# Wide attention with its score tile in 3 + 1 PSUM banks, its exponential in two instructions, and a new instruction order

## The chip, the core and the metric

One NeuronCore of a Trainium2 chip runs the whole program. The metric is the device time in microseconds (us) of one execution, as the median of several. The engines run side by side and meet only at semaphores: TensorE (PE in the profile) multiplies matrices into PSUM, ScalarE (ACT) computes exponentials and copies, VectorE (DVE) copies and does elementwise work, GpSimd (POOL) copies within SBUF and issues DMAs, SyncE (SP) issues DMAs. PSUM is eight banks, each of 512 fp32 numbers on each of 128 partitions; a matmul's result of 512 columns fills a bank.

## The reference, cut to what matters

Two attentions read the same input `x` (2048 x 576), and a gate mixes them.

```python
# A: 64 segments of 32 rows, one after the other; 8 memory rows go from one to the next
for s in range(n_seg):
    h = concatenate([mem, xs])                 # 8 + 32 rows
    q, k, v = h @ Wq, h @ Wk, h @ Wv           # 32 heads of 128
    p = softmax(where(mask, q @ k.T * scale, -1e9))
    o = (p @ v) @ Wo
    mem, out_s = o[:, :M], o[:, M:]
# B: plain attention over all 2048 rows, 32 heads of 18
b = softmax(q @ k.T * Dh ** -0.5) @ v @ wo
return g * a + (1 - g) * b                     # g = sigmoid(sum(x * gate_w))
```

A is a recurrence: segment s + 1 needs the output of segment s. B, the wide attention, has no such chain but 32 score matrices of 2048 x 2048, and so nearly all of the exponentials.

## The kernel before, in words

**Stages.** First x is transposed and B's q, k and v are projected (`xt`, `pq`, `pv`, L580 to L751) and written to DRAM. Then A's 64 segments run one after the other, and B's attention is laid between their steps. Last come B's output product and the mix (L1667, L1683).

**The wide attention.** B's heads are taken in 8 groups of 4, the queries in 4 chunks of 512, the keys in 16 blocks of 128: 32 x 16 = 512 *visits* (loops over `gq` and `kb`). A visit has three steps:

- `sb` (L906): four matmuls, one for each head, on four row tiles of PE, into one tile `sb` of 128 x 4 x 512 fp32, which is four PSUM banks;
- `ex` (L915): one exponential on ACT over all 2048 columns into the SBUF tile `etb` (two buffers);
- `ob` (L924): four matmuls on four column tiles that add the values, weighted, into `ob`, a bank which stays open for 16 visits.

There is one `sb` tile, so the scores of the next visit can't start before the exponential of this one has ended. The other three banks are a common pool, `pb`, from which everything else takes its PSUM.

**A segment of the recurrence.** `Q`, `K`, `V` (L1249) project the 40 rows in two halves each, copies bring them to SBUF (`tm`, L520 on ACT or L522 on DVE), q and k are turned by a DMA transpose (L1340) and copied (L1349). For each half follow `ph` (scores, L1364 and L1372), an exponential on ACT (L1382), `sm` (sums, L1396), a reciprocal (L1408), `bc` (spread, L1422), a product (L1433), `po` (values, L1444, two pool banks at once), copies `ot`, and `op` (output product, L1157). `fo` (L1501) forms the next segment's memory rows. The last 8 rows of each segment don't feed the recurrence and are projected ahead (`la`, L994 and L998).

**What sets the order.** No scheduler of the compiler does: the class `Plan` does, while the program is built. Each step is added with an engine (or a choice of two), a modelled duration, its dependences, a priority, and the tokens (PSUM banks, buffers) that it takes and gives back. `run` then places steps one at a time on the engine that is free first, by priorities that are weighed anew at each segment by a number from the list `TURNS`. Each engine then runs its steps in exactly that order. The steps of PE have a *mode* (row, col, tall, full: how the array is tiled). Where the plan leaves PE idle for long, it places filler matmuls (`warm`, L877, zeros added to the open `ob`). A visit may not run ahead of the recurrence by more than a share: each later `sb` also depends on a step of some segment (`seg_gate`).

Of the kernel before, what the change touches and what calls it, by code (L numbers as in the profile page):

```python
# [10 lines left out]
FP32 = mybir.dt.float32  # L11
BF16 = mybir.dt.bfloat16
ACT = mybir.ActivationFunctionType
# [41 lines left out]
]  # L55
RANK = dict(RANKS[0])
TURNS = [
    7943601, 1705423, 4803270, 706643, 9682343, 8274704, 7872199, 5071302, 3371851, 3273616, 4640218, 4495581,
    5292743, 3779423, 6345635, 4968460, 6155672, 9072000, 3125259, 7567437, 7423799, 1541135, 1346239,
    9763583, 3431211, 1894600, 9694456, 752252, 1250417, 1686256, 2185370, 1863123, 9947015, 7980497, 9379971,  # L60
    9658427, 1322130, 8351749, 3131186, 1013253, 3672070, 1863938, 4951784, 5438165, 9176668, 3266295,
    9739128, 9697170, 3740036, 3789983, 7951007, 3736728, 7365096, 2930305, 1889627, 3969272, 8605176, 949486,
    6403568, 927810, 5200634, 8113583, 1742827, 48857, 9352253,
]
FACTORS = (0.02, 0.1, 0.25, 0.4, 0.55, 0.7, 0.85, 1.0, 1.2, 1.5, 1.9, 2.4, 3.0, 4.0, 6.0, 10.0)
KNOBS = ("switch", "near", "early", "wait", "gap", "cool")
# [10 lines left out]


def kind_of(name):
    if re.match(r"(sb|ob|ex)\d+\.", name):  # L80
        return name[:2]
    if re.match(r"l[ae]\d", name):
        return name[:2] + ("v" if name.split(".")[1] == "2" else "q")
    m = re.match(r"([a-zA-Z]+\d?)\.\d+(?:\.\d+)?$", name) or re.match(r"([a-zA-Z]{2})\d+$", name)
    return m.group(1) if m else "x"
# [20 lines left out]
class Plan:  # L106
# [57 lines left out]
    def add(  # L164
        self, name, engs, dur, fn, deps=(), prio=5.0, mode=None, take=(), give=(), tail=0.0, dmas=0, kb=0.0,
        use=None, pairs=4,
    ):
        op = Op(name, engs, dur, fn, deps, prio, mode, take, give, tail)
        op.dmas, op.kb = dmas, kb
        op.pairs = pairs  # L170
        op.kind = self.kinds.setdefault(kind_of(name), len(self.kinds))
        op.use = self.ARRAY.get(mode) if use is None else use
        op.seq = len(self.ops)
        op.slots = {}
        self.ops.append(op)
        return op
# [179 lines left out]
def act_time(n):  # L356
    return (n + 205) / 1200.0
# [3 lines left out]
def kernel(  # L361
# [15 lines left out]
    nc = tc.nc  # L377
    P = nc.NUM_PARTITIONS
# [12 lines left out]
    QC = 512  # L391
# [16 lines left out]
    scale_b = float(DhB) ** -0.5  # L408
# [6 lines left out]
    plan = Plan()  # L415
    add = plan.add
# [29 lines left out]
    for jj in range(2):  # L446
        nc.vector.memset(bsel[64 * jj:64 * jj + 64, jj:jj + 1], 1.0)
    nc.gpsimd.affine_select(
        out=veil[0:64, M:L], in_=veil[0:64, M:L], pattern=[[1, seg]],
# [3 lines left out]
        out=veil[0:64, 0:M], in_=veil[0:64, 0:M], pattern=[[0, M]],  # L453
        compare_op=ALU.is_gt, fill=-30000.0, base=L, channel_multiplier=-1,
    )
    for j in range(4):
        r = slice(32 * j, 32 * j + 32)
# [41 lines left out]
    ps_s = ctx.enter_context(tc.tile_pool(name="ps_s", bufs=1, space=psum))  # L499
# [1 line left out]
    ps_a = ctx.enter_context(tc.tile_pool(name="ps_a", bufs=1, space=psum))  # L501
    plan.tokens_of("sb", 1)
    plan.tokens_of("ob", 1)
    plan.tokens_of("pb", 3)
    plan.tokens_of("etb", 2)

    def bank(shape, dt, name, k=0):
        return ps_a.tile(shape, dt, name=name, tag=f"pb{plan.slot('pb', k)}")
# [48 lines left out]
    box = {}  # L557
# [229 lines left out]
    def gate(e):  # L787
        pgs = bank([P, NT], FP32, "pgs")
        for n in range(NT):
            for c in range(NF + 1):  # L790
# [7 lines left out]
             prio=0.45, mode="full", take=("pb",), pairs=80)  # L798
# [38 lines left out]
    k_of, v_of, q_of = {}, {}, {}  # L837
# [35 lines left out]
    last_vi = last_va = None  # L873
# [16 lines left out]
    for gq in range(GB * NQC):  # L890
        RANK.update(RANKS[gq // 8])
        g, qc = divmod(gq, NQC)
        load_q(gq)
        for kb in range(NKB):
            c = 4 * g + kb // KC
            o = (kb % KC) * P
            if qc == 0 and kb % KC == 0:
                load_k(c)
                load_v(c)

            def visit(e, c=c, gq=gq, o=o, kb=kb):
                box["sb", gq, kb] = sb = ps_s.tile([P, 4, QC], FP32, name="sb")
                kc, qt_ = kring[c % NKR], qring[gq % NQR]
                for j in range(4):
                    r = slice(32 * j, 32 * j + 32)
                    nc.tensor.matmul(  # L906
                        sb[:, j, :], lhsT=kc[r, o:o + P], rhs=qt_[r, :], start=True, stop=True,
                        tile_position=(32 * j, 0),
                    )

            vi = add(f"sb{gq}.{kb}", "PE", 0.216, visit, [k_of[c], q_of[gq], last_vi], prio=-0.6 if gq < 2 else 0.0, mode="row", take=("sb",))

            def expo(e, gq=gq, kb=kb):
                box["etb", gq, kb] = etb = given(bint, "etb", [P, 4, QC], BF16)
                nc.scalar.activation(out=etb[:, :, :], in_=box["sb", gq, kb][:, :, :], func=ACT.Exp, scale=scale_b)  # L915

            ex = add(f"ex{gq}.{kb}", "ACT", act_time(2048), expo, [vi], prio=0.0, take=("etb",), give=(("sb", vi, 0),))

            def values(e, c=c, gq=gq, kb=kb, o=o):
                if kb == 0:  # L920
                    box["ob"] = ps_o.tile([P, QC], FP32, name="ob")
                ob, vc, etb = box["ob"], vring[c % NVR], box["etb", gq, kb]
                for j in range(4):
                    nc.tensor.matmul(  # L924
                        ob[32 * j:32 * j + 32, :], lhsT=vc[:, o + 32 * j:o + 32 * j + 32], rhs=etb[:, j, :],
                        start=(kb == 0), stop=(kb == NKB - 1), tile_position=(0, 32 * j), skip_group_check=True,
                    )
                if kb == NKB - 1:
                    box["ob", gq] = ob

            va = add(
                f"ob{gq}.{kb}", "PE", 0.216, values, [ex, v_of[c], last_va], prio=-0.5 if gq < 2 else RANK["ob"], mode="col",
                take=("ob",) if kb == 0 else (), give=(("etb", ex, 0),),
            )
            visits[gq, kb] = (vi, ex, va)
            last_vi, last_va = vi, va
            if kb == 0:
                plan.opens.add(va)
            if kb == NKB - 1:
                plan.closes.add(va)  # L940
            if kb == 0:
                first_va = va
            if kb == NKB - 1:
                visits["quse", gq] = vi
            if qc == NQC - 1 and kb % KC == KC - 1:
                visits["kuse", c], visits["vuse", c] = vi, va

        NBK = QC // 32

        def f_turn(e, gq=gq):  # L950
            box["tq", gq] = tq = bint.tile([P, NBK, 32], FP32, name="tq")
            nc.vector.transpose(out=tq[:, :, :].rearrange("p b e -> p (b e)"), in_=box["ob", gq][:, :])

        def f_rec(e, gq=gq):
            box["rtb", gq] = rtb = bint.tile([P, NBK, 1], FP32, name="rtb")
            nc.vector.reciprocal(out=rtb[:, :, :], in_=box["tq", gq][:, :, DhB:DhB + 1])

        def f_mul(e, gq=gq):
            box["tn", gq] = tn = bint.tile([P, NBK, 32], BF16, name="tn")
            nc.vector.tensor_tensor(  # L960
                out=tn[:, :, :], in0=box["tq", gq][:, :, :],
                in1=box["rtb", gq][:, :, :].to_broadcast([P, NBK, 32]), op=ALU.mult,
            )

        def f_back(e, gq=gq):
            box["stage", gq] = stage = bint.tile([P, QC], BF16, name="stage", bufs=2)
            nc.vector.transpose(out=stage[:, :], in_=box["tn", gq][:, :, :].rearrange("p b e -> p (b e)"))  # L967

        prev = fin_state.get("back")
        f1 = add(f"ft{gq}", "DVE", 0.7, f_turn, [va, prev], prio=0.5, give=(("ob", first_va, 0),))  # L970
        f2 = add(f"fr{gq}", "DVE", 0.26, f_rec, [f1], prio=RANK["fin"])
        f3 = add(f"fm{gq}", "DVE", 0.7, f_mul, [f2], prio=RANK["fin"])
        store2 = stages.get(gq - 2)
        f4 = add(f"fb{gq}", "DVE", 0.7, f_back, [f3, store2], prio=RANK["fin"])
        fin_state["back"] = f4
        if gq < GB * NQC - 1:
            def f_store(e, gq=gq, g=g, qc=qc):
                by_head(otd, g, slice(qc * QC, (qc + 1) * QC), box["stage", gq], True, queue(e))

            stages[gq] = add(f"fs{gq}", *carrier(4, True), f_store, [f4], prio=0.9, dmas=4, kb=90)  # L980
        else:
            stages[gq] = f4
# [196 lines left out]
    for s in range(n_seg):  # L1179
# [45 lines left out]
        def ld_v(e, s=s):  # L1225
# [8 lines left out]
            prio=0.76, dmas=2, kb=64,  # L1234
# [70 lines left out]
        for hf in range(2):  # L1305
# [3 lines left out]
            for a, ev_a in ((0, eq), (1, ek)):  # L1309
                if hf in ON_PE:  # L1310
                    def turn_pe(e, hf=hf, s=s, a=a):
# [11 lines left out]
                        take=("pb",), give=(("tm", ev_a, 0),), pairs=16,  # L1323
# [14 lines left out]
                def turn(e, hf=hf, s=s, a=a):  # L1338
# [5 lines left out]
                    give=(("tm", ev_a, 0),), dmas=1, kb=128,  # L1344
                )

                def ct(e, hf=hf, s=s, a=a):
# [8 lines left out]
                    prio=RANK["ct"], give=(("tt", t_, 0),),  # L1356
# [31 lines left out]
            def sm(e, hf=hf, s=s):  # L1388
                box["pss", s, hf] = ps = bank([P, 6], FP32, "pss")
                for k, o in enumerate(CH):  # L1390
# [4 lines left out]
                    for i in range(4) if SM_COL else ():  # L1395
# [7 lines left out]
                     mode="col" if SM_COL else "full", take=("pb",), use=0.05, pairs=12 if SM_COL else 3)  # L1403
# [33 lines left out]
            def pso(e, hf=hf, s=s):  # L1437
# [3 lines left out]
                for r in range(8):  # L1441
                    for jj in range(2):
# [8 lines left out]
                     give=(("tm", evx, 0),))  # L1451
# [292 lines left out]
```

## Time and profile before

| | |
|---|---|
| median of 3 runs | 1467.89 us (1466.71 to 1469.4) |
| the profiled execution, a fourth one | 1462.26 us |
| its span, first to last instruction | 1460.4 us |
| PE, ACT, DVE, POOL busy | 1364.7, 1055.9, 793.9, 556.3 us |
| exponential of a visit on ACT | 512 x 1877 ns |
| ACT idle just before it | 317.0 us |
| first `sb`, last `sb` start | 63.6 us, 1445.2 us |
| filler matmuls on PE | 768 in column tiles (192 fours), 2 whole |

All other numbers are of the profiled execution. A busy share counts the time in which an instruction of the engine is recorded; on PE the records overlap, since one matmul starts while the one before still drains. A group's line gives line number, engine, operation, output and input tiles, shapes and count, then busy time and mean ns of one, then how long the engine stood idle just before such an instruction and who ended that. `[0.61 <-ACT etb L915]` in a timeline means: idle for 0.61 us, until ACT's instruction of line 915 that writes `etb` was done.

### The profile page before, as it was taken

To read this page: it belongs to the slowest core of one execution; us is meant where nothing else is said; L and a number is where in the kernel's file an instruction comes from. 1 tells how busy PE (TensorE), PEld (TensorE's weight loads), DVE (VectorE), ACT (ScalarE), POOL (GpSimd) and SP (SyncE) were. 2 spreads that over 40 slices of the span, in tenths; PEclk is the share of its full clock that TensorE was granted. 3 is DMA by queue.
4 is the path that set the end of the run, shared out by engine and by line. 5 is a ranking of instruction groups with operands and counts; after the bars stand their busy time and mean duration, and the time that the engine had idled before them with its cause. 6 is when DMAs were issued, how large, how long until landed. Compare 5 with 4: busy or idle time off the path is not lost.

```text
span 1460.4 us, 79019 instructions
## 1 busy us (share of the span) xinstructions
PE 1364.7 (93%) x35726; PEld 760.8 (52%) x35735; DVE 793.9 (54%) x1862; ACT 1055.9 (72%) x773; POOL 556.3 (38%) x1194
## 2 busy tenths in 40 slices
PE   6889999999999999999999999999998999988998
PEld 4446455555555545555555455555554454544544
DVE  6434555656566555555555565555554555555554
ACT  2257677777877777777777777887777778777884
POOL 6323336333453335333454334541444342523210
PEclk9999999999999999999999999999999999999999
DMA  8986534333324233333233333333343323332261
GB/s 251 323 273 197 106 71 76 68 60 74 74 70 74 57 69 76 66 59 72 56 86 67 67 67 68 82 63 65 62 94 63 57 53 57 71 59 56 48 166 59
DMA packets 343420, 130.75 MB, mean 90 GB/s; under 512 B 296943, under 2 KB 329159, under 8 KB 343083
## 3 DMA queue, kind: packets, MB, share of 16 engines
q1 hardware_dynamic: 314771, 81.20, 27.7%
q0 software_dynamic: 27088, 43.31, 10.6%
q8 instruction: 279, 4.57, 1.4%
q10 hardware_dynamic: 1224, 1.20, 0.2%
q14 instruction: 58, 0.48, 0.1%
HBM read 52.74 MB, written 30.86 MB: 57 GB/s over the span
## 4 chain that ended last, share of the span: by engine, by line
PE 60%; DMA 6%; DVE 6%; ACT 6%; issue 4%; POOL 1%; ACTq 0%; DVEq 0%; POOLq 0%
PE pvv L1249 22%; PE acc L1157 8%; PE sb L906 8%; PE ob L924 7%; DMA tt<-tm 5%; ACT etb L915 5%; PE pv L994 3%; PE pso L1444 2%; PE ob L877 2%; PE po L1667 1%; PE prb L1422 1%; DVE tm L522 1%; DMA v_sb<-tm 1%; PE psh L1372 1%; PE pw L1501 1%
## 5 line engine op out<-in xcount | busy, mean ns | idle before, releaser
L915 ACT ACTIVATE etb<-sb 128x2048 bf16<-128x2048 f32 x512 | 961.2, 1877 | 317.0 <-PE sb L906 304.0
L522 DVE CAST tm<-pvv 128x512 bf16<-128x512 f32 x364 | 251.1, 690 | 255.2 <-PE pvv L1249 248.2
L1249 PEld LDWEIGHTS <-ht 128*32 128x32 bf16 x7680 | 202.1, 96 | 194.8 <-DVE ht L1511 19.8
L906 PE MATMUL sb<-qch,kch 32*128 32x512 bf16 x2048 | 204.0, 385 | 13.9 <-ACT etb L915 10.7
L924 PE MATMUL ob<-etb,vch 128*32 128x512 bf16 x2048 | 203.4, 388 | 1.0 <-issue 0.6
L1157 PE MATMUL acc<-wo,ot 128*32 128x144 bf16 x8192 | 165.8, 227 | 9.5 <-issue 7.8
L1157 PEld LDWEIGHTS <-ot 128*32 128x32 bf16 x8192 | 136.3, 96 | 34.6 <-issue 14.5
L1249 PE MATMUL pvv<-wk_m,ht 128*32 128x512 bf16 x2048 | 142.2, 379 | 0.3 <-DVE ht L1511 0.3
L1249 PE MATMUL pvv<-wq_m,ht 128*32 128x512 bf16 x2048 | 137.4, 380 | 3.8 <-DVE ht L1511 0.6
L1249 PE MATMUL pvv<-wv_m,ht 128*32 128x512 bf16 x2048 | 140.0, 379 | 0.4 <-DVE tm L522 0.4
L906 PEld LDWEIGHTS <-kch 32*128 32x128 bf16 x2048 | 59.7, 91 | 140.4 <-issue 114.3
L522 DVE CAST ot<-pso 128x320 bf16<-128x320 f32 x197 | 90.9, 486 | 72.4 <-PE pso L1444 70.4
L826 POOL DMA_DIRECT2D qch<-qtd x120 | 61.8, 522 | 108.2 <-PE sb L906 107.5
L1349 DVE COPY qk<-tt 128x512 bf16<-128x512 bf16 x256 | 80.7, 322 | 32.5 <-DMA tt<-tm 29.5
L924 PEld LDWEIGHTS <-vch 128*32 128x32 bf16 x2048 | 53.4, 93 | 81.2 <-issue 76.3
L1200 POOL COPY ht<-xg 128x96 bf16<-128x96 bf16 x64 | 18.0, 281 | 203.1 <-PE pvv L1249 201.9
L1288 POOL COPY v_sb<-tm 32x512 bf16<-32x512 bf16 x68 | 42.8, 629 | 126.3 <-DVE tm L522 111.6
L826 POOL DMA_DIRECT2D otd<-stage x124 | 62.9, 514 | 58.5 <-DVE stage L967 35.2
L1433 DVE TENSOR_TENSOR et<-et,prb 128x320 bf16<-128x320 bf16 x128 | 62.0, 484 | 36.4 <-PE prb L1422 34.1
L826 POOL DMA_DIRECT2D kch<-ktd x112 | 57.2, 518 | 59.0 <-PE sb L906 49.4
L522 DVE CAST vl<-pv 128x512 bf16<-128x512 f32 x86 | 58.7, 685 | 34.2 <-PE pv L994 23.4
L1382 ACT ACTIVATE et<-psh 128x320 bf16<-128x320 f32 x128 | 55.7, 435 | 13.3 <-PE psh L1372 12.2
(152 smaller groups left out, 1853.4 us busy)
## 6 DMA issues: line engine op xcount, KB each, us to landing
xl<-qkd SPq DMA_DIRECT2D x64, 128.0 KB
v_sb<-tm SPq DMA_DIRECT2D x256, 32.0 KB
qkd<-vl POOLq DMA_DIRECT2D x48, 128.0 KB, 2.3
wo<-in_A_Wo_dram POOLq DMA_DIRECT2D x4, 1152.0 KB
vgd<-vt SPq DMA_DIRECT2D x32, 128.0 KB
wv_m<-in_A_Wv_dram POOLq DMA_DIRECT2D x4, 1024.0 KB, 7.0
wq_m<-in_A_Wq_dram POOLq DMA_DIRECT2D x4, 1024.0 KB, 7.5
wk_m<-in_A_Wk_dram POOLq DMA_DIRECT2D x4, 1024.0 KB, 8.1
```

The costliest lines, as they stand in the source:

```text
L522: nc.vector.tensor_copy(out=out_of(), in_=in_of())
L826: dma(out=rows_, in_=pads) if out else dma(out=pads, in_=rows_)
L906: nc.tensor.matmul(sb[:, j, :], lhsT=kc[r, o:o + P], rhs=qt_[r, :], start=True, stop=True, tile_position=(32 * j, 0),)
L915: nc.scalar.activation(out=etb[:, :, :], in_=box["sb", gq, kb][:, :, :], func=ACT.Exp, scale=scale_b)
L924: nc.tensor.matmul(ob[32 * j:32 * j + 32, :], lhsT=vc[:, o + 32 * j:o + 32 * j + 32], rhs=etb[:, j, :], start=(kb == 0), stop=(kb == NKB - ...
L994: nc.tensor.matmul(out_, lhsT=lw, rhs=rw, start=(c == 0), stop=(c == NF))
L1157: nc.tensor.matmul(acc[32 * j:32 * j + 32, :], lhsT=o[:, slot, t0:t0 + CT], rhs=wo[:, h, RW * j:RW * j + RW], start=(first and s_ == 0), s ...
L1249: nc.tensor.matmul(pv[32 * j:32 * j + 32, :], lhsT=ht[:, cc, :], rhs=rw, start=(c == 0), stop=(c == NF), tile_position=(0, 32 * j), skip_g ...
L1288: move(out=opened["v_sb"][64 * (j // 2):64 * (j // 2) + CT, o:o + 512], in_=tm[32 * j:32 * j + CT, :],)
L1349: eng.tensor_copy(out=opened["qk"][:, hf, a, 0:16 * L].rearrange("p (j i t) -> p j i t", i=4, t=L)[:, :, :, 0:CT], in_=box["tt", s, a, hf] ...
L1382: nc.scalar.activation(out=opened["et", hf][:, :], in_=box["psh", s, hf][:, :], func=ACT.Exp, scale=scale_a)
L1433: nc.vector.tensor_tensor(out=et[:, :], in0=et[:, :], in1=box["prb", s, hf][:, :], op=ALU.mult)
```

## The change

The score tile has three banks instead of four. The fourth head's scores go to a bank `sp` of the common pool, which grows from three to four. The exponential is two instructions: three heads (1536 columns), which gives back the three banks, then one head (512), which gives back the pool's bank. The values wait for both. The list `TURNS` is another one, so the order of all steps on all engines differs. Lines after the change stand 6 lower than before from L936 on (L1249 becomes L1255), `sb` is L907, `ob` L930, the two exponentials L916 and L920.

```diff
@@ TURNS = [
-    7943601, 1705423, 4803270, 706643, 9682343, 8274704, 7872199, 5071302, 3371851, 3273616, 4640218, 4495581,
...
+    7483491, 5720459, 7783898, 6678073, 6223742, 3115698, 6578494, 0, 354389, 7990747, 1981828, 1088679,
...
-    plan.tokens_of("pb", 3)
+    plan.tokens_of("pb", 4)
...
-                box["sb", gq, kb] = sb = ps_s.tile([P, 4, QC], FP32, name="sb")
+                box["sb", gq, kb] = sb = ps_s.tile([P, 3, QC], FP32, name="sb")
+                box["sp", gq, kb] = sp = bank([P, QC], FP32, "sp")
...
                     nc.tensor.matmul(
-                        sb[:, j, :], lhsT=kc[r, o:o + P], rhs=qt_[r, :], start=True, stop=True,
+                        sb[:, j, :] if j < 3 else sp[:, :], lhsT=kc[r, o:o + P], rhs=qt_[r, :], start=True, stop=True,
                         tile_position=(32 * j, 0),
                     )
-            vi = add(f"sb{gq}.{kb}", "PE", 0.216, visit, [k_of[c], q_of[gq], last_vi], prio=-0.6 if gq < 2 else 0.0, mode="row", take=("sb",))
+            vi = add(f"sb{gq}.{kb}", "PE", 0.216, visit, [k_of[c], q_of[gq], last_vi], prio=-0.6 if gq < 2 else 0.0, mode="row", take=("sb", "pb"))
...
-                nc.scalar.activation(out=etb[:, :, :], in_=box["sb", gq, kb][:, :, :], func=ACT.Exp, scale=scale_b)
-
-            ex = add(f"ex{gq}.{kb}", "ACT", act_time(2048), expo, [vi], prio=0.0, take=("etb",), give=(("sb", vi, 0),))
+                nc.scalar.activation(out=etb[:, 0:3, :], in_=box["sb", gq, kb][:, :, :], func=ACT.Exp, scale=scale_b)
+
+            def expo4(e, gq=gq, kb=kb):
+                etb = box["etb", gq, kb]
+                nc.scalar.activation(out=etb[:, 3, :], in_=box["sp", gq, kb][:, :], func=ACT.Exp, scale=scale_b)
+
+            ex = add(f"ex{gq}.{kb}", "ACT", act_time(1536), expo, [vi], prio=0.0, take=("etb",), give=(("sb", vi, 0),))
+            ey = add(f"ey{gq}.{kb}", "ACT", act_time(512), expo4, [ex], prio=0.01, give=(("pb", vi, 0),))
...
             va = add(
-                f"ob{gq}.{kb}", "PE", 0.216, values, [ex, v_of[c], last_va], prio=-0.5 if gq < 2 else RANK["ob"], mode="col",
+                f"ob{gq}.{kb}", "PE", 0.216, values, [ex, ey, v_of[c], last_va], prio=-0.5 if gq < 2 else RANK["ob"], mode="col",
                 take=("ob",) if kb == 0 else (), give=(("etb", ex, 0),),
             )
```

The modelled durations in `add` and `act_time` steer the order only; nothing of them runs. Counted in the two programs as they are built:

| | before | after |
|---|---|---|
| matmuls on PE | 35735 | 35767 |
| fillers (fours) | 192 | 200 |
| changes of PE's mode | 1356 | 1382 |
| exponentials of the wide attention | 512 | 1024 |
| copies `tm` on DVE, on ACT | 364, 20 | 343, 41 |
| copies `vl` on DVE, on ACT | 86, 10 | 78, 18 |
| copies `v_sb` on DVE, on POOL | 188, 68 | 208, 48 |

## The prediction

> **What bounds the kernel now.** First the page: span and busy shares, then the slices.
>
> ```profile
> span 1460.4 us, 79019 instructions
> PE 1364.7 (93%) x35726; PEld 760.8 (52%) x35735; DVE 793.9 (54%) x1862; ACT 1055.9 (72%) x773; POOL 556.3 (38%) x1194
> ...
> PE   6889999999999999999999999999998999988998
> ACT  2257677777877777777777777887777778777884
> ```
>
> The tensor engine is the only one near full, from slice 4 to the end; ScalarE stands at seven tenths throughout. An engine at a constant seven tenths is either paced by another or waits in every round for the same thing, so next the groups and the waits of the wide attention.
>
> ```profile
> L915 ACT ACTIVATE etb<-sb 128x2048 bf16<-128x2048 f32 x512 | 961.2, 1877 | 317.0 <-PE sb L906 304.0
> L906 PE MATMUL sb<-qch,kch 32*128 32x512 bf16 x2048 | 204.0, 385 | 13.9 <-ACT etb L915 10.7
> L924 PE MATMUL ob<-etb,vch 128*32 128x512 bf16 x2048 | 203.4, 388 | 1.0 <-issue 0.6
> ```
>
> Each waits for the other: the exponential for the scores (304 us, on an engine with room), the scores for the exponential (10.7 us shown, on the engine without room). The timeline shows the ring, first on PE, then on ACT.
>
> ```profile
> 1140.10 0.39 PE L906 MATMUL sb<-qch,kch 32*128 32x512 bf16 x4
> 1140.43 0.40 PE L924 MATMUL ob<-etb,vch 128*32 128x512 bf16 x4
> 1140.74 1.18 PE L1157 MATMUL acc<-wo,ot 128*32 128x144 bf16 x64
> 1142.54 0.40 PE L906 MATMUL sb<-qch,kch 32*128 32x512 bf16 x4 [0.61 <-ACT etb L915]
> ```
>
> ```profile
> 1140.61 1.88 ACT L915 ACTIVATE etb<-sb 128x2048 bf16<-128x2048 f32 x1
> 1143.04 1.88 ACT L915 ACTIVATE etb<-sb 128x2048 bf16<-128x2048 f32 x1 [0.56 <-PE sb L906]
> ```
>
> The four score banks are one tile. Its ring takes 0.51 us from the scores' start to the exponential's start, 1.88 for the exponential, 0.05 back to PE: 2.43 (here 1142.54 - 1140.10 = 2.44). PE stood 0.61 us, with ready work behind the waiting matmul. The windows say where this is worst.
>
> ```profile
> 876.00:1022.00 146.00, 141.79 (x4048) 83.66 (x4047) 78.87 (x188) 113.98 (x88) 57.96 (x124) 1.00 0.34 70
> 1022.00:1168.00 146.00, 133.23 (x3804) 73.20 (x3800) 76.59 (x180) 110.65 (x81) 62.56 (x131) 1.00 0.37 69
> 1168.00:1314.00 146.00, 132.46 (x3992) 72.12 (x3988) 76.17 (x182) 114.68 (x86) 57.38 (x123) 1.00 0.34 60
> ```
>
> The first number after the length is PE's busy time: 142 of 146 us up to 1022, 133 and 132 after that.
>
> **What the Trainium skill says.** "Perfetto Trace Analysis", Identifying the Most-Contended Engine: matmul busy time is no good measure of what is left, since matmuls overlap. The trace agrees: a wait of 0.1 us hides under the end of the matmul before, so I count from start to start below. The same page, Identifying Performance Opportunities: a bubble that repeats can mean that PSUM has no room for the next tile; the 0.56 us above is such a bubble (no gap between two successive exponentials was shorter than 0.55). The same page, Optimizing Scalar/DVE Operations: where ScalarE is not full but makes others wait, instructions may be broken up, at about 51 ns of engine time each for PSUM; the trace gives 65, worked out below, and that is used. "TensorE: Matmul & The Clock Gate", Part 3: matmuls start and end strictly in order, so all that is queued behind a waiting one waits too. The 0.61 us agree.
>
> **The floor.** I laid out PE's order of the program before and gave each step its undisturbed start-to-start time from the trace: 0.216 us for four column- or row-tiled matmuls of 512, 0.25 for 16 of `acc`, 0.36 for a `psh`, 0.17 for a `prb`, and 0.105 for every change of tiling (scores to values take 0.32, not 0.216). It sums to 1282.6 us; the other 177.8 of the span is PE standing: 34 before the first segment of the recurrence (DMA busy at eight to nine tenths there), 12 at the end and in the drain, and 131 in the segments. There 52 us stand before score and value matmuls (42.8 and 9.7), and 58 before the recurrence's own steps (`sm`, `bc`, `po`, `op`, `fo`, `Q0`, `ph`).
>
> In the order of the changed program the same prices give 1287.1: 202 filler quads instead of 194 (8 x 0.216 = 1.7) and 1382 changes of tiling instead of 1356 (26 x 0.105 = 2.7). **Plus 4.5.** Nothing else on PE differs in kind or number.
>
> **The exponential in two parts.** The 320-wide `exp` takes 435 ns, the 2048-wide 1877, so 0.8345 ns an element: 1450 for three heads, 595 for one. Neighbours on ACT overlap by 103 ns (median of 114 pairs). The pair takes 1450 + 595 - 103 = 1942, 65 more than now; 512 x 0.065 = 33 us of ACT, which has 400 free, so on the path it costs only what the values wait longer. The ring of the three banks becomes 0.51 + 1.45 + 0.05 = 2.00 instead of 2.43, while the second part runs in the 0.56 us bubble. What ACT loses is that bubble as a place for its other work (21 more `tm` and 8 more `vl` copies go to it, 29 x 0.48 = 14 us). Over any run of eight visits of the new order ACT's work fits between the matmuls that bracket it, so I add 2 us for local queueing.
>
> **The waits that follow.** A wait costs where PE's order puts too little work between a step and the next that needs it. For each visit I took this cover (floor time between the two starts) in both orders. Before, the next scores need 2.43 and the visit's values 2.43: of each visit the larger shortfall, summed, is 61.4 us (198 visits), nearly all of it scores; the trace shows 52.5, so 0.85 of it is paid. After, the scores need 2.00, the values 0.51 + 1.94 + 0.06 = 2.51, and whoever takes the pool bank that the fourth head held needs 2.51 too. The shortfalls sum to 53.0: scores 10.7, values 22.0, the bank 20.2. So the scores' wait goes, and most of it comes back as two waits at the second part. Queued behind the values are all column-tiled steps; behind the bank's taker, most often the next scores' fourth matmul (29 visits) or a `po` (27 times). **Gain 0.85 x 8.4 = 7.** Bounds: with needs 0.05 lower the sum is 42 (gain 16), with 0.1 more 74 (loss 11).
>
> **The recurrence's steps.** Same count, with needs as the trace shows them when such a step was late: `ph` to `sm` 1.13, `sm` to `bc` 0.56, `bc` to `po` 1.00, `po` to `op` 1.01 and 0.93, `op` to `fo` 0.84, `fo` to `Q0` 0.58, `K` to `ph` 5.0, `V` to `po` 4.6. Shortfalls now 55.7, in the new order 36.4; without `V` to `po` and `K` to `ph`, which are partly the same waits as others of the list, 35.3 against 26.9. Seen: 58. **Gain 14**, between 8 and 19. This is the new order's share: visits are no longer tied to 2.43, so steps can lie further apart.
>
> **What moves without cost.** Issues on SP and POOL are equal in number; 20 `v_sb` copies go from POOL (629 ns) to DVE (297), 21 `tm` and 4 `vl` copies leave DVE for ACT. DVE at 54% hides that; without cover each would cost its 0.3 us, 6 in all. Before the visits begin the pool has four banks, not three; transfers set that stage, so nothing, at best 5.
>
> **Sum.** Against the profiled execution (1462.3 us, span 1460.4): + 4.5 + 2 - 7 - 14 = -14.5, and half of the start's possible 5, together -17. The shown runs have a median of 1467.9, 5.6 above the profiled one; I take the difference over: 1451.
>
> **The rivals.** (a) The orders were laid out with less slack than the banks now give and PE makes use of all of it: the scores' 42.8 us go but for the bank's 20, the values stay, and the recurrence gains 19: 1467.9 - 23 - 19 + 4.5, about 1430. For it: after 1022 us, where PE is worst, the shortfalls fall most (23 to 15 in the last fifth of the visits). Against: the values' shortfall doubles. (b) The waits only move: the visits lose the upper bound's 11, the recurrence gains 11, and with 4.5 more floor, less the start's 3: 1467.9 to 1470; no change. (c) Slower: the bank. The fourth head holds a pool bank for 2.51 us, and visits come every 2.7 (1382 us from the first to the last of 512), so one of the four is nearly always gone and at a quick hand-over two. A `po` takes two banks at once; if in each of 64 segments PE stands 0.7 us, one eviction of 690 ns, for a bank which used to be free, that is 45 us, against 17: 1496. It decides from 17 / 64 = 0.27 us per segment. Against it: eviction covers in the new order are no shorter than now (medians 1.2 to 1.7 us).
>
> **Numbers.** 1451 case 0.60; (a) 0.17; (b) 0.11; (c) 0.12. The first case's own range is 1440 to 1464. The range, 1429 to 1470, leaves out half of (a) and (c). A measurement here tells about 0.2% (3 us) from no change: faster than 1465 0.77, within 0.10, slower 0.13.
>
> **What would show it.** Right: three-head exponentials of 1.45 us, gaps on ACT under 0.1 us after the second part where the ring is tight; scores waiting for ACT well below 10.7 us, values and `po` waiting for ACT where now nothing is listed; PE's busy share after 1022 us nearer 97%. Wrong: the two parts don't overlap by 0.1 us (values' need 2.61, gain gone), or PE's waits for DVE at `sp` and `po` exceed 20 us.

## The result, and the profile after

| | before | after |
|---|---|---|
| median, runs | 1470.29 us, 20 (1464.6 to 1477.24) | 1475.53 us, 20 (1464.6 to 1485.05) |
| ratio of the two | | 1.0028, 95% interval 1.0008 to 1.0048 |
| the profiled execution, its span | 1462.26, 1460.4 us | 1476.89, 1475.1 us |
| from the first projection of the recurrence to the end | 1311.2 us | 1320.2 us |

The change made the kernel slower, by about 4 us (the ratio; the medians are 5.2 apart), where 17 less were forecast. The profiled execution of before was quicker than all 20 of these runs, so the spans are further apart than the medians. Of all runs told of below one, of the shortened kernel before, counts as slow and is left out of its median and ratio. A second profile of each kernel (the first experiment) has 1313.8 and 1322.9 us in the last row: the recurrence and everything beside it takes 9 us longer. Ahead of it lies a stage bound by transfers, which took between 149 and 160 us in these four profiles, and in which two profiles of each can't show a difference.

The same views as before, the page first.

```profile
span 1475.1 us, 79537 instructions
PE 1375.4 (93%) x35767; PEld 753.3 (51%) x35767; DVE 775.5 (53%) x1856; ACT 1098.7 (74%) x1311; POOL 541.7 (37%) x1174
...
q8 instruction: 279, 4.57, 1.4%
...
L916 ACT ACTIVATE etb<-sb 128x1536 bf16<-128x1536 f32 x512 | 743.4, 1452 | 234.9 <-PE sp L907 184.8
L920 ACT ACTIVATE etb<-sp 128x512 bf16<-128x512 f32 x512 | 304.9, 596 | 0.7 <-PE sp L907 0.7
L907 PE MATMUL sb<-qch,kch 32*128 32x512 bf16 x1536 | 201.6, 386 | 4.4 <-ACT etb L916 3.6
L930 PE MATMUL ob<-etb,vch 128*32 128x512 bf16 x2048 | 203.5, 384 | 1.5 <-issue 1.1
```

The exponentials are what the forecast said: 1452 and 596 ns, and no idle time before the second part. The pair takes 1939 ns in the middle case, 62 more than the one instruction. The scores wait 3.6 us for ACT instead of 10.7. ACT's timeline shows the ring where it is tight.

```profile
1112.68 1.45 ACT L916 ACTIVATE etb<-sb 128x1536 bf16<-128x1536 f32 x1 [0.23 <-PE sp L907]
1114.03 0.59 ACT L920 ACTIVATE etb<-sp 128x512 bf16<-128x512 f32 x1
```

The second part starts at 1114.03, 0.10 us before the first has ended (1112.68 + 1.45 = 1114.13). All this came as forecast, and PE's waits show where the gain isn't. The first fence is after, the second before; columns: who waited and for whom, us in all, how often, the longest.

```profile
PE acc L1163 <- issue: 20.6, 30, 1.5
PE psh L1378 <- DVE qk L1355: 10.7, 15, 1.7
...
PE prb L1428 <- issue: 4.0, 3, 1.6
...
PE sb L907 <- ACT etb L916: 3.6, 11, 0.6
```

```profile
PE acc L1157 <- issue: 11.1, 21, 1.4
PE sb L906 <- ACT etb L915: 10.7, 29, 0.9
...
PE psh L1372 <- DVE qk L1349: 4.0, 10, 0.8
```

Seven us of waiting for ACT went, and eleven of "issue" came (21.5 us in before's whole list, 32.4 in after's). `psh` waits longer as well, for the turned q and k: 4.0 us in before (6.5 in its second profile), 10.7 in after (9.9). "issue" is a wait for nothing that the profile shows. In before's timeline it looks like this, in the middle of a group of 16 matmuls that need nothing new:

```profile
1138.47 0.32 PE L1444 MATMUL pso<-et,v_sb 64*128 64x40 bf16 x11
1139.94 0.23 PE L1444 MATMUL pso<-et,v_sb 64*128 64x40 bf16 x5 [1.15 <-issue]
```

Eleven of the 16 run, PE stands for 1.15 us, and the other five run. I gave each matmul of the trace its place in PE's program as built (71558 instructions before, 71605 after, nearly all of them two to a matmul: its weight load and itself). Divided by 256, the places of these gaps leave the same remainder, 193 to 195, in both. And the instruction queue of PE, q8 on the page, moved 279 packets and 4.57 MB, in both: 16 KB each, and 71558 / 256 = 279.5. **PE ran out of instructions.** A block of 256 comes as one packet; the packet takes about 1.1 us, no two start less than 3.25 us apart in any run (in before one in ten less than 3.54), and PE goes on 1.43 us after a late packet's end, in the middle case. Blocks of PE's work that ended in such a gap took about 3.75 us in the middle case, in before and in after. That isn't a fixed limit: one block in ten passed in 3.5 us or less, the shortest of before in 2.7. But where PE goes through 256 instructions much faster than 3.75 us, block after block, it waits for the next one. Counted from start to start at these places, less the prices of the forecast's floor, this standing is:

| | fetch, us | blocks that came late |
|---|---|---|
| before, again | 35.0, 36.1 | 57, 58 of 274 |
| after, again | 52.5, 53.1 | 76, 76 |

It is more than the "issue" of the list (32.4 for after), which counts only from the end of the last matmul and leaves out gaps with another releaser named.

"Runtime: NRT & Kernel Launch" of the Trainium skill, Instruction fetch mechanics, has the 256 instructions and 16 KiB to a block, and the trace agrees; it also says that crossing a block's boundary is mostly hidden, since instructions are issued more slowly than fetched. For PE in these kernels the trace says otherwise: one boundary in five of before and more than one in four of after isn't hidden, and the measurement decides.

### The profile page after: what moved, and what is told of

Read it like the earlier page. It is cut to its first block, busy times and chain, and to the rows that moved or that the text cites. A ratio compares the mean times of both kernels' runs of the same rounds, so it can differ in the third digit from the quotient of the medians.

```text
span 1475.1 us, 79537 instructions
## 1 busy us (share of the span) xinstructions
PE 1375.4 (93%) x35767; PEld 753.3 (51%) x35767; DVE 775.5 (53%) x1856; ACT 1098.7 (74%) x1311; POOL 541.7 (37%) x1174
## 3 DMA queue, kind: packets, MB, share of 16 engines
q8 instruction: 279, 4.57, 1.4%
## 5 line engine op out<-in xcount | busy, mean ns | idle before, releaser
L916 ACT ACTIVATE etb<-sb 128x1536 bf16<-128x1536 f32 x512 | 743.4, 1452 | 234.9 <-PE sp L907 184.8
L522 DVE CAST tm<-pvv 128x512 bf16<-128x512 f32 x343 | 236.3, 689 | 237.3 <-PE pvv L1255 233.8
L1255 PEld LDWEIGHTS <-ht 128*32 128x32 bf16 x7680 | 198.1, 96 | 223.8 <-issue 42.8
L920 ACT ACTIVATE etb<-sp 128x512 bf16<-128x512 f32 x512 | 304.9, 596 | 0.7 <-PE sp L907 0.7
L907 PE MATMUL sb<-qch,kch 32*128 32x512 bf16 x1536 | 201.6, 386 | 4.4 <-ACT etb L916 3.6
L930 PE MATMUL ob<-etb,vch 128*32 128x512 bf16 x2048 | 203.5, 384 | 1.5 <-issue 1.1
L907 PE MATMUL sp<-qch,kch 32*128 32x512 bf16 x512 | 197.3, 385 | 6.9 <-DVE wo L634 2.0
L1255 PE MATMUL pvv<-wk_m,ht 128*32 128x512 bf16 x2048 | 148.6, 381 | 0.5
L1255 PE MATMUL pvv<-wv_m,ht 128*32 128x512 bf16 x2048 | 145.0, 380 | 0.1
L1255 PE MATMUL pvv<-wq_m,ht 128*32 128x512 bf16 x2048 | 141.7, 381 | 2.7 <-DVE ht L1517 0.6
L907 PEld LDWEIGHTS <-kch 32*128 32x128 bf16 x2048 | 54.4, 91 | 140.8 <-issue 124.2
L930 PEld LDWEIGHTS <-vch 128*32 128x32 bf16 x2048 | 54.4, 94 | 58.3 <-issue 48.7
L522 DVE CAST vl<-pv 128x512 bf16<-128x512 f32 x78 | 53.4, 688 | 37.2 <-PE pv L1000 17.4
```

Of the source, the lines that this page charges most:

```text
L522: nc.vector.tensor_copy(out=out_of(), in_=in_of())
L907: nc.tensor.matmul(sb[:, j, :] if j < 3 else sp[:, :], lhsT=kc[r, o:o + P], rhs=qt_[r, :], start=True, stop=True, tile_position=(32 * j, 0),)
L916: nc.scalar.activation(out=etb[:, 0:3, :], in_=box["sb", gq, kb][:, :, :], func=ACT.Exp, scale=scale_b)
L920: nc.scalar.activation(out=etb[:, 3, :], in_=box["sp", gq, kb][:, :], func=ACT.Exp, scale=scale_b)
L930: nc.tensor.matmul(ob[32 * j:32 * j + 32, :], lhsT=vc[:, o + 32 * j:o + 32 * j + 32], rhs=etb[:, j, :], start=(kb == 0), stop=(kb == NKB - ...
L1255: nc.tensor.matmul(pv[32 * j:32 * j + 32, :], lhsT=ht[:, cc, :], rhs=rw, start=(c == 0), stop=(c == NF), tile_position=(0, 32 * j), skip_g ...
```

## The experiments

Theory: the waits that the change takes away lie in stretches where PE's 256 instructions go by in about the time that a block takes to fetch, so fetch takes the place of the wait. Rivals: the second part itself costs it, by the values that wait for it or by the pool bank that it holds; or the list of turns was searched for something that isn't there on the chip.

### With fewer instructions on PE

Both kernels as they are, and both with fewer instructions in about the same PE time: the 32 `psh` matmuls of 40 columns become two fours of 320 and 208 (more columns than before, yet from a `psh` to the next step's start it takes 0.47 us either way, in the middle case), each 16 `acc` matmuls of 144 become fours of 512 and 64. So 16384 of PE's 71558 instructions are left out; the sums of those columns are not those of the recurrence, and only the time is read. All four ran on one chip.

```diff
-                    state["acc"] = bank([P, RW], FP32, "acc")
+                    state["acc"] = bank([P, 512], FP32, "acc")
-                for s_ in range(lo, lo + 4):
+                for s_, w in ((lo, 512), (lo + 3, 64)):
...
-                            acc[32 * j:32 * j + 32, :], lhsT=o[:, slot, t0:t0 + CT],
-                            rhs=wo[:, h, RW * j:RW * j + RW],
+                            acc[32 * j:32 * j + 32, 0:w], lhsT=o[:, slot, t0:t0 + CT],
+                            rhs=wo[:, h, 0:w],
...
-                for r in range(8):
+                for w in (W8, 208):
...
-                            ph[32 * i:32 * i + 32, r * L:(r + 1) * L],
+                            ph[32 * i:32 * i + 32, 0:w],
...
```

> The kernel before once more, for a second profile and as the control of this group. Ratio to itself 1.000 within 0.003. In its first profile PE stood about 31 us at steps of 256 instructions of its own program (a place that drifts with nothing else): if this is the fetch of PE's instructions, the second profile shows 31 +- 8 us at the same places; if it was chance, the places differ.

> The changed kernel once more. Ratio 1.001 to 1.005. Fetch theory: again clearly more standing at steps of 256 PE instructions than the kernel before (49 us in the first profile, expected 40 to 55). Rival (the waits only moved to the values and the pool's bank): standing before values and bank takers makes up the whole difference and the steps of 256 show no more than before.

> The kernel before with 8192 fewer matmuls (and weight loads) on PE in the same order and about the same PE time: per half segment the 32 head products of the recurrence's scores are replaced by 8 wide ones, and each 16 matmuls of its output product by one four of 512 and one of 64 columns; so A's scores and output are computed from the wrong pairs and this part of the computation is changed. 215 blocks of 256 instructions instead of 279, and by the prices used before hardly any block is passed in under 3.75 us. Fetch theory: 25 to 45 us faster (1425 to 1445), the standing at steps of 256 gone. Rival: within 5 us of the kernel before.

> The same replacement (A's scores and output product computed from the wrong pairs) in the changed kernel, its order kept. Fetch theory: with the fetch out of the way the gain that was forecast shows: 8 to 18 us faster than the kernel before with the same replacement. Rival, waits moved to values and bank: still as much slower than its counterpart as the changed kernel is now, 2 to 8 us.

Measured, as ratios to the kernel before on this chip (1469.87 us, 39 runs):

| | median, us | ratio, 95% interval | fetch, us |
|---|---|---|---|
| before again | 1471.09 | 1.0007 [0.9988, 1.0026] | 36.1 |
| after again | 1476.93 | 1.0047 [1.0029, 1.0065] | 53.1 |
| before, few | 1447.46 | 0.9846 [0.9793, 0.9899] | 5.8 |
| after, few | 1435.74 | 0.9772 [0.9740, 0.9804] | 4.7 |

With the fetch nearly gone the sign turns: after is now about 11 us ahead, 0.9772 / 0.9846 = 0.9925 with about 0.006 either way from the two intervals, so between 2 and 20. The first projection to the end agrees: 1286.4 and 1273.1 us. So without fetch the change gains; the interval holds the 17 that were forecast, and less. Before itself gained 22 us from the shorter program, a little less than the 25 to 45 that I had expected. The waits of the first, then of the second short version:

```profile
PE sb L906 <- ACT etb L915: 16.7, 38, 1.2
PE psh L1372 <- DVE qk L1349: 9.0, 16, 0.9
...
PE pq L712 <- issue: 0.4, 2, 0.2
```

```profile
PE psh L1378 <- DVE qk L1355: 9.3, 16, 1.8
...
PE sb L907 <- ACT etb L916: 5.3, 15, 0.7
...
PE pvb L751 <- issue: 0.8, 1, 0.8
PE pq L712 <- issue: 0.4, 2, 0.2
```

The score wait, 10.7 us in before, is 16.7 without fetch: more of it shows where PE no longer stands for instructions. Of "issue" the two lists hold 0.6 and 1.5 us.

In the full kernels the places add up. Of some 273 blocks 133 are dense in both orders (under 3.75 us by the floor's prices). They took 505 and 508 us in the two profiles of before, 503 and 514 after, 3.8 to 3.9 us a block each time; other waits in them fell from 65 or 66 to between 43 and 55, fetch rose from 35 to between 50 and 52. In the other blocks waits rose, from 37 to 39 to between 45 and 54. The two profiles of after differ by some ten us in this division, so it is rough. A simpler difference is firmer, the time from the first projection to the end less the fetch: 1276.2 and 1277.7 us in the two profiles of before, 1267.7 and 1269.8 in those of after. So everything else takes 8 us less, and fetch 17 more. Most of the rise stands within `acc`: 17 and 19 us of fetch there before, 32 and 31 after.

### The exponential's wait taken away from the kernel before

The same test from the other side: the score banks free sooner with before's order and nothing else changed. The exponential covers three heads of four (1.45 us), and the fourth head's values use the third's weights, so a quarter of the exponentials is left out.

```diff
-                nc.scalar.activation(out=etb[:, :, :], in_=box["sb", gq, kb][:, :, :], func=ACT.Exp, scale=scale_b)
+                nc.scalar.activation(out=etb[:, 0:3, :], in_=box["sb", gq, kb][:, 0:3, :], func=ACT.Exp, scale=scale_b)
...
-                        ob[32 * j:32 * j + 32, :], lhsT=vc[:, o + 32 * j:o + 32 * j + 32], rhs=etb[:, j, :],
+                        ob[32 * j:32 * j + 32, :], lhsT=vc[:, o + 32 * j:o + 32 * j + 32], rhs=etb[:, min(j, 2), :],
```

> The kernel before, its order and banks kept, but the wide attention's exponential covers three heads (1536 columns) and the values of the fourth head are taken with the third head's weights; the fourth head's exponential is left out. The ring of the scores falls from 2.43 to 2.00 us and nothing else changes, so of 61 us of shortfall 14 are left: with 0.85 paid, 40 us faster (32 to 45) if nothing takes the wait's place. Fetch theory: the fetch takes over part of it, 10 to 25 us faster, and the standing at steps of 256 PE instructions rises from 30 us to 38 to 55.

> The same shorter exponential (fourth head's left out) together with the 8192 fewer matmuls of the recurrence's scores and output product (computed from the wrong pairs). Fetch theory: with the fetch gone the shorter ring pays in full, 28 to 45 us faster than the kernel before with the fewer matmuls alone (1449), so 1404 to 1421. Rival (the ring is worth 10 to 25 whatever the fetch does): 1424 to 1439.

Measured, on a chip with the kernel before at 1461.35 us (30 runs): 1454.42 us, 0.9957 [0.9932, 0.9981], and with fewer instructions 1426.47, 0.9750 [0.9722, 0.9778]. Against the short before (0.9846, on the other chip) that is 0.9903, some 14 us. The wait is gone in both (3.3 and 5.1 us of the ring, against 22.6 and 31.9), and 426 ns of ACT a visit with it. In the full kernel that gave 6 us, less than either forecast: its dense blocks took 499 us (505 before). And the fetch didn't rise to 38 to 55: it is 36.5, against 35.0 and 36.1. In the short one the gain is 14, within some 9 either way, not the 28 to 45 of my theory but what I had written down for the rival, 10 to 25 whatever the fetch does; that it is more than the 6 isn't clear of the noise. So half of the ring's wait or more came back as other waits with and without fetch. Counted start to start, the waits before the recurrence's steps rose by some 11 us in the full kernel and 6 in the short one; the list of the short one, which begins so, shows little of that (before the change of its exponential the two lines stood at 7.7 and 9.0).

```profile
PE prb L1422 <- DVE rq L1408: 8.0, 17, 1.0
PE psh L1372 <- DVE qk L1349: 7.2, 12, 2.0
```

The theory is thus half right. Fetch is what makes after the slower one, but a wait that goes isn't always replaced by fetch: with before's order the wait went and the fetch stayed.

### Fewer instructions with nothing left out

The `psh` scores on two column tiles of 64 instead of four of 32: 18 matmuls a half instead of 36, the same products.

```diff
-                for i in range(4):
-                    o = 32 * (i % 2)
+                for i in range(2):
...
-                            ph[32 * i:32 * i + 32, r * L:(r + 1) * L],
-                            lhsT=qk[:, hf, 1, k * L + o:k * L + o + 32], rhs=qk[:, hf, 0, k * L:(k + 1) * L],
-                            start=False, stop=True, tile_position=(0, 32 * i), skip_group_check=True,
+                            ph[64 * i:64 * i + 64, r * L:(r + 1) * L],
+                            lhsT=qk[:, hf, 1, k * L:k * L + 64], rhs=qk[:, hf, 0, k * L:(k + 1) * L],
+                            start=False, stop=True, tile_position=(0, 64 * i), skip_group_check=True,
```

> The changed kernel with the recurrence's scores on two column tiles of 64 instead of four of 32: the same products in 18 matmuls instead of 36 for each half segment, so 2304 matmuls and as many weight loads fewer (18 blocks of 256 instructions of 279), nothing left out. Fetch theory: 5 to 15 us faster than the changed kernel if going from 32-wide to 64-wide tiles and back costs nothing. If each such change costs the 0.105 us of the other changes of tiling, 256 of them add 27 us, and it ends 10 to 20 us slower.

Measured: 1467.20 us, 1.0041 [1.0027, 1.0055], where after stood at 1.0028 and 1.0047. PE's program fell to 67070 instructions, q8 to 262 packets, the fetch from 53 to 30.6 us (51 blocks of 257). The time didn't move. Two matmuls of a `psh` now take turns where four ran side by side, and 256 times a kernel PE changes from tiles of 32 to tiles of 64 or back; I put the lost 22 us down to these. The trace fits: from the start of the matmul before a `psh` to its first matmul 0.31 us pass instead of 0.21 in the middle case, 11 us in all, and the `psh` steps take 5 us more in all; no run has one without the other. Neither of the two forecasts, a gain of 5 to 15 and a loss of 10 to 20, came. It gives no version that beats before.

### The two lists of turns exchanged

```diff
 TURNS = [
-    7483491, 5720459, 7783898, 6678073, 6223742, 3115698, 6578494, 0, 354389, 7990747, 1981828, 1088679,
+    7943601, 1705423, 4803270, 706643, 9682343, 8274704, 7872199, 5071302, 3371851, 3273616, 4640218, 4495581,
...
```

> The changed kernel with the list of the kernel before, so banks and exponential are split but the order wasn't searched for them. If the order is what matters: 5 to 30 us slower than the changed kernel, since the list fits another set of banks. If the split itself does the work and the list is indifferent: within 5 us of the changed kernel.

> The kernel before with the changed kernel's list, so one tile of four banks, one exponential, and an order not searched for them. If a list fits only the structure it was searched for: 50 us or more slower than the kernel before, as the reverse exchange was 140. If the new list is better in itself: within 10 us or faster.

Measured: the split structure with before's list 1601.0 us, 1.0947 [1.0915, 1.0979]; before's structure with the new list 1594.33, 1.0918 [1.0878, 1.0958]. They are 140 and 134 us slower, the first far outside both ranges that I had given. Each of the two lists is good only for the structure that it was searched with: the priorities of one segment act on a state of the plan that the next differs in. So the diff can't be split into "banks" and "order" by undoing one; the pair must be judged. The search of the new list is not at fault as such, since with fewer instructions its order and banks together are the faster pair.

### The second part taken out of the values' way, and shortened

In after: the fourth values use the third head's weights, so no value matmul waits for the second part; then also the second part over 64 columns instead of 512, so that it gives its pool bank back sooner. Parts of the fourth head are left out in both.

```diff
-                        ob[32 * j:32 * j + 32, :], lhsT=vc[:, o + 32 * j:o + 32 * j + 32], rhs=etb[:, j, :],
+                        ob[32 * j:32 * j + 32, :], lhsT=vc[:, o + 32 * j:o + 32 * j + 32], rhs=etb[:, min(j, 2), :],
```

```diff
-                nc.scalar.activation(out=etb[:, 3, :], in_=box["sp", gq, kb][:, :], func=ACT.Exp, scale=scale_b)
+                nc.scalar.activation(out=etb[:, 3, 0:64], in_=box["sp", gq, kb][:, 0:64], func=ACT.Exp, scale=scale_b)
```

> The changed kernel, order kept, but the fourth head's values are taken with the third head's weights (that head's result is left out of the computation), so no value matmul waits for the second part of the exponential; the pool's bank is still held until its end. By the shortfalls of the forecast (53.0 to 42.0) 9 us faster than the changed kernel. By what its trace shows inside the value fours just after the second part (4.1 us) 0 to 4 us faster.

> As the last one, and the second part of the exponential covers 64 columns instead of 512 (the rest left out), so the pool's bank comes back 0.37 us earlier and ACT has 190 us less to do. By the shortfalls of the forecast (53.0 to 28.2) 21 us faster than the changed kernel. By its trace (2.6 us of scores waiting just after the second part, 4.1 in the value fours), and with the fetch taking its share of what goes, 2 to 7 us faster.

Measured, with before at 1460.56 us (43 runs): 1461.35, 1.0006 [0.9988, 1.0024], and 1462.32, 1.0007 [0.9988, 1.0026]. After stood at 1.0028 and 1.0047, so both give some 3 to 6 us (against the first of the two figures this isn't clear of the noise), and the shorter hold of the bank gives nothing on top. The second part costs little: the values' wait for it is worth about 4 us, the bank nothing that shows.

## Why the prediction was wrong

**The step that failed is the floor:** "It sums to 1282.6 us; the other 177.8 of the span is PE standing", with the 131 in the segments laid to the banks, the values and the recurrence. 35 of it was PE standing for instructions. No term of the sum held it, though before's own list of waits had it in first place and one line that I copied, the values', ends in "<-issue 0.6". A floor of single prices assumes that PE can run at them one after the other; the blocks of 256 instructions that came late took 3.75 us in the middle case, and 133 blocks are priced at less. In after this standing is 17 us longer, and nothing in the forecast stood against it: with all else 8 us shorter it makes the gain a loss of 9. Why it rose isn't shown. That the fetch took the place of the waits explains it in part at most, since 17 is more than what went elsewhere, and in before with the shorter exponential the wait went and the fetch stayed. What is left is the new order, or the split beyond its shorter ring; no run separates the two.

**The scores' stall, "42.8 before score matmuls":** only 22.6 of it was released by the exponential; 16 was fetch in the step just ahead of the scores. The term that I called "0.85 is paid" was fitted to a sum which had other things in it. In after the exponential's share is 7.2: the real gain is 15.4.

**The values, 22 us, and the bank, 20:** too large and of another kind. Only the fourth value matmul waits for the second part, so before the values after finds 4.1 us, and their removal gave about 4. Inside the fours of scores 11 us stand (`sp` wants a pool bank), of which 2.6 directly after a second part; the rest are banks that DVE frees. About +4 and +10.5. That is the third rival's mechanism at a quarter of its price; DVE's share of it is read from the trace, no run tested it.

**The recurrence, gain 14:** too large, and wrong for one step. Net of fetch its steps' waits fell from 42.2 and 39.2 us to 30.2, about 11, in a first count; a count of every step from its start to the next one's gives about 6: 9 less before `sm`, `bc`, `po`, `op` and `fo`, 2 less before the projections, but 5 more before `ph`. The lists of waits say the same of `ph`, for the turned q and k: 4.0 and 6.5 us before, 10.7 and 9.9 after, where the shortfalls from `K` to `ph` should have become smaller. The 58 that I saw held fetch too.

**Right as written:** 1450 and 595 ns, the overlap of 0.10 us, the scores' wait well below 10.7. The 4.5 of floor was not measured by itself. A `po` waits for ACT's second part 0.7 us in all, the values by no line of the list. **The window** didn't come: after 1022 us PE's share rose, from 133.2 and 132.5 us of 146 to 137.1 and 134.4, not to 97%, and before 1022 it fell, from 141.8 to 135.1.

```profile
876.00:1022.00 146.00, 135.14 (x3844) 76.51 (x3840) 76.15 (x184) 111.62 (x135) 61.83 (x130) 1.00 0.42 68
1022.00:1168.00 146.00, 137.09 (x3900) 75.29 (x3897) 74.08 (x181) 111.29 (x131) 57.93 (x123) 0.99 0.36 69
1168.00:1314.00 146.00, 134.36 (x3820) 70.63 (x3820) 75.64 (x188) 108.25 (x126) 46.08 (x102) 1.00 0.34 58
```

**The sum again,** with what was measured: +4.5 floor, -15.4 scores, +4 values, +10.5 bank, -6 recurrence, +17 fetch: +14.6, beside the +9 from the first projection to the end. The terms were each counted by themselves, one of them 3 us apart in two profiles of one kernel, so the sum shows which are large and no more. The medians, +5.2 and on the second chip +5.8, lie lower by what the start may have given; I forecast 2.5 there, and its scatter of 11 us leaves that open. The +2 for queueing on ACT is not seen as a term of its own.

Of the rivals, (b), "the waits only move", came nearest: its time, 1467.9 to 1470, but not its mechanism. What remains open: why the fetch rose by 17 us, though by the prices as many blocks are dense, and what makes the waits of the recurrence come back where the ring's wait goes.

## What to carry to other kernels

Before a wait on a full engine is counted as gain, count that engine's instructions: here the standing gaps at steps of 256 instructions, and one packet on the instruction queue for each, showed that PE's own program held it up at one block in five, and after the change at more than one in four. A gap marked "issue" in the middle of a group that needs nothing new points to the number of instructions; with 23% of them left out the same change went from 4 us slower to 11 us faster (2 to 20). And a sum of single prices against a span shows how much an engine stands, not for whom: each part needs its releaser before it is put into a term.

## What the runs showed of the hardware

- PE's instructions came in blocks of 256, one packet of 16 KB each, never less than 3.25 us apart in any run, and in the four profiles of before and after fewer than one in ten less than 3.5; PE went on 1.43 us (half of them 1.3 to 1.5) after a late one's end. At 3.5 us that is some 14 ns an instruction, 28 a matmul with its load, while a `psh` (36 matmuls in 0.36 us) takes 10 ns for each matmul and 16 `acc` matmuls (0.25 us) 16: blocks full of either run ahead of the fetch.
- An exponential of 2048 columns cut into 1536 and 512 cost ACT 62 to 67 ns more, with neighbours overlapping by 104.
- With half as many `psh` matmuls, on column tiles of 64, the kernel took as long as with those on tiles of 32, though the fetch fell by 22 us.
